# Spectral layer, expert layer and MLP on one core: the bias added after the sums, clipping and stores placed one class pair later, router logits from float32 token tiles

## The chip, the cores and the metric

The kernel runs on one core of a Trainium2 chip. The metric is the device time of one execution in microseconds (us). Three runs of the kernel before gave 3658.37, 3660.32 and 3661.04 us; the median is 3660.32 us. About 0.2% (7 us) can be told from no change in this kernel.

## The reference, cut to what matters

Three layers follow one another over eight sequences of 3072 tokens of 256 features. The first goes to the frequency domain along the sequence, multiplies by a complex 256x256 matrix, adds a complex bias, shrinks by 0.01 towards zero and goes back. The second sends each token with a positive skip score to one of eight experts. The third is a two-layer MLP with a leaky activation.

```python
X = np.fft.rfft(x, axis=1)
Yr = X.real @ w_r - X.imag @ w_i + b_r
Yi = X.real @ w_i + X.imag @ w_r + b_i
Yr = np.sign(Yr) * np.maximum(np.abs(Yr) - lam, 0.0)      # Yi likewise
x = np.fft.irfft(Yr + 1j * Yi, n=3072, axis=1)            # (8, 3072, 256)
...
xc = x[x @ w_skip > 0]
logits = xc @ w_gate                                      # 8 experts, the largest one is used
...
h = x @ w_in
return (np.maximum(h, 0.0) + alpha * np.minimum(h, 0.0)) @ w_out
```

The product with the complex matrix and the experts' products are done with float32 operands split into two float32r parts, high and low.

## The kernel before, in words

**Stages.** The transforms are factored as 3072 = 48 x 64. Stage A (`A_mm`) multiplies a 96-row input tile by a 96x96 matrix and stores the result to DRAM (`sA`). Stage B (`B_mm`) loads 128-row tiles `S` from there and multiplies by the second factor, two frequency classes at a time. `mix` multiplies by the complex weights, `shrink` adds the bias and shrinks, `C_mm` starts the way back and stores to DRAM (`sZ`), and `D_mm` finishes it into token tiles `xo`, which go to DRAM (`xb`). `T_tr` transposes each token tile, `T_mm` computes the skip score and the eight logits, `route` makes list positions of them in some ten pieces, and `scatter` writes list entries by indirect DMAs from GpSimd, 24 a batch.

**The order.** The loop runs over 97 steps; a step is one class pair of a batch (twelve pairs a batch, pair number `pp`). The schedule is written out by hand: each engine executes its instructions in the order of the program text. Step s issues the loads for s+2, then `B_mm` of pair s+1, then `T_mm` of a waiting token tile, one A, D or transposing unit as a filler, the list scatters (two a step, from step 72 four), `mix` of pair s with more fillers between its sums, `shrink` of pair s, and `C_mm` of pair s-1. A batch of inputs costs 16 A units, issued some batches ahead: two a step in pairs 11, 0, 1 and 2, one in the others, and none after step 76. A batch's 16 D units go two a step in pairs 3 to 10 of the batch after it. After the 97 steps the experts' stage begins at line 712; the last batch's D units, transposes and logits run inside it (`tail_step`).

**Three products.** For pairs other than 0, `B_three` makes three operands (`m`): real and imaginary part by one copy on ScalarE (line 213) and their sum `xs`, which is added on VectorE (line 214), rounded on ScalarE (line 215) and whose low part is taken on GpSimd (line 217). `mix_three` forms k1 from the sums and k2 and k3 from the parts. Line 232 copies k1 to `u` on ScalarE, and line 234 adds the two biases to it on GpSimd and writes `ub`. `shrink` then adds `ub` to k2 and k3 on VectorE in four 64x256 pieces (line 272), clips (274) and subtracts (275).

**Logits.** `T_tr` keeps the transposed token tile as a high part `th` (ScalarE, line 317) and a low part `tl` (VectorE, line 318). `T_mm` holds the router's weights stationary and streams 384 tokens past them four times; four tiles gather in one PSUM bank, and line 332 transposes that bank in 32x32 blocks.

**Buffers.** The pool `pa` has four PSUM banks and a step takes four (B, k1, k2 and k3 together, C), so each use gets the bank of the same use one step earlier. `pb` has three banks for A, D and transposes. `y`, `zc`, `sa` and `zin` have two buffers, `xo` and `xin` three.

Of the kernel before, what the change touches and what calls it, by code (L numbers as in the profile page):

```python
# [21 lines left out]
NQ, NP = 32, 96  # L22
# [21 lines left out]
def _constants():  # L44
# [42 lines left out]
    g, i = p // 32, p % 32  # L87
    q = 16 * (r // 12) + 4 * g + (r % 12) // 3
    tok = (X0 + SEQ * b + 32 * (32 * (r % 3) + i) + q).astype(np.float32)
# [10 lines left out]
def spectral_moe_mlp(ctx, tc, x, w_r, w_i, b_r, b_i, w_skip, w_gate, w1, w2,  # L100
# [28 lines left out]
    if True:  # L129
# [6 lines left out]
        bias = cp.tile([128, 4, D], F32, name="bias")  # L136
# [3 lines left out]
        wgw = tp.tile([128, 2, 224], F32R, name="wgw")  # L140
# [14 lines left out]
        def A_mm(b, u):  # L155
            q = bank(pb)
            nc.tensor.matmul(q[:96], agt[:, 0], xin[b, u // 2][:, 2 * (u % 2):2 * (u % 2) + 2, :], start=True, stop=True)
            if u % 2 == 0:
                sast[b] = p2.tile([96, 4, D], F32, name="sa")
            dst, src = sast[b][:, 2 * (u % 2):2 * (u % 2) + 2, :], q[:96].rearrange("p (a d) -> p a d", d=D)  # L160
            t = sast[b]
            nc.scalar.copy(dst, src)
            if u % 2 == 1:
                ch = u // 2
                for rj in range(4):
                    nc.sync.dma_start(sA[b % 3][rj, 4 * ch:4 * ch + 4].rearrange("q c d -> c q d"),
                                      t[24 * rj:24 * rj + 24])
# [34 lines left out]
        def B_three(src, m, pp):  # L202

            q = bank(pa).rearrange("p (k j i f) -> p k j i f", k=2, j=2, i=2)
            for i in range(2):
                for kt in range(2):
                    nc.tensor.matmul(q[:, kt, :, i], src[:, i, 128 * kt:128 * kt + 128], fct[:, 2 * pp + i],
                                     start=True, stop=True)
            q = q.rearrange("p k j i f -> p k j (i f)")
            xi = p2.tile([128, 2, 128], F32, name="xi", bufs=1)  # L210
            xs = p2.tile([128, 2, 128], F32, name="xs")
            nc.scalar.copy(xi, q[:, :, 1])
            nc.scalar.copy(m[:, :, 0, 0:2], q)
            nc.vector.tensor_tensor(out=xs, in0=q[:, :, 0], in1=xi, op=add)
            nc.scalar.copy(m[:, :, 0, 2], xs)  # L215
            nc.vector.tensor_tensor(out=m[:, :, 1, 0:2], in0=q, in1=m[:, :, 0, 0:2], op=sub)
            nc.gpsimd.tensor_tensor(out=m[:, :, 1, 2], in0=xs, in1=m[:, :, 0, 2], op=sub)  # L217

        def mix_three(b, pp, fill):
# [3 lines left out]
            for o, j, w in ((k1, 2, 0), (k23[:, 0], 1, 2), (k23[:, 1], 0, 1)):  # L223
# [12 lines left out]
            Y[b, pp] = (k23, ub)  # L236
# [24 lines left out]
        def shrink(b, pp):  # L261
            q = Y[b, pp]
            y = p2.tile([128, 2, D], F32, name="y")
            if pp == 0:
                for i in range(2):
                    nc.vector.tensor_tensor(out=y[:, i], in0=q[:, i], in1=bias[:, 3 - i], op=add)
            else:
                q, ub = q
                for i in range(2):
                    for j in range(2):  # L270
                        r = slice(64 * i, 64 * i + 64)
                        nc.vector.tensor_tensor(out=y[64 * j:64 * j + 64, i], in0=q[r, j], in1=ub[r, j], op=add)  # L272
# [3 lines left out]
            Y[b, pp] = y  # L276

        def C_mm(b, pp):
# [5 lines left out]
            nc.scalar.copy(z, q)  # L284
            for rj in range(4):
# [8 lines left out]
        def D_mm(b, u):  # L294
# [7 lines left out]
            if u % 2 == 1:  # L302
                nc.sync.dma_start(
                    xb[X0 + SEQ * b:X0 + SEQ * b + SEQ].rearrange("(p q) d -> p q d", q=NQ)[:, 4 * ch:4 * ch + 4, :], t)
# [3 lines left out]
        def T_tr(b, ch, kt):  # L308
            src = xo[b, ch]
            if kt == 0:  # L310
                xt[b, ch] = (t2.tile([128, 2, 384], F32R, name="th", bufs=1),
                             t2.tile([128, 2, 384], F32R, name="tl", bufs=1))
            h, l = xt[b, ch]
# [3 lines left out]
            nc.scalar.copy(h[:, kt], q[:, :384])  # L317
            nc.vector.tensor_tensor(out=l[:, kt], in0=q[:, :384], in1=h[:, kt], op=sub)

        def T_mm(b, ch):  # L320
            h, l = xt.pop((b, ch))
            g = ch % 4
            if g == 0:
                lgt[b] = bank(pc)
            q = lgt[b][:, :384]
            for kt in range(2):
                wv = wgw[:, kt, 96 - 32 * g:224 - 32 * g]
                nc.tensor.matmul(q, wv, h[:, kt], start=(g == 0 and kt == 0), stop=False)
                nc.tensor.matmul(q, wv, l[:, kt], start=False, stop=(g == 3 and kt == 1))
            if g == 3:  # L330
                lt = t2.tile([128, 12, 32], F32, name="lt")
                nc.vector.transpose(out=lt.rearrange("p a c -> p (a c)"), in_=q)
                if ch == 3:
                    sal[b] = t2.tile([128, 24, 9], F32, name="sal")
                nc.vector.tensor_tensor(out=sal[b][:, 3 * ch - 9:3 * ch + 3], in0=lt[:, :, 0:9], in1=lt[:, :, 9:18], op=add)
# [247 lines left out]
        def setup0():  # L583
# [7 lines left out]
            nc.sync.dma_start(bias[:, 0], bcast(b_r, 128))  # L591
            nc.sync.dma_start(bias[:, 1], bcast(b_i, 128))
            nc.sync.dma_start(bias[0:64, 2], bcast(b_r, 64))
            nc.sync.dma_start(bias[64:128, 2], bcast(b_i, 64))
            nc.sync.dma_start(bias[0:65, 3], bcast(b_r, 65))
            nc.sync.dma_start(bias[65:128, 3], bcast(b_i, 63))
# [7 lines left out]
        def setup2():  # L604
            V = nc.vector
            for kt in range(2):
                V.tensor_copy(wgw[:, kt], zero[:, 0:224])
            V.tensor_copy(wgw[:, :, 96:105], gst)
            V.tensor_tensor(out=wgw[:, :, 105:114], in0=gst, in1=wgw[:, :, 96:105], op=sub)
# [8 lines left out]
            pad = padt[0] = t2.tile([128, LS // 256, 3], I32, name="pad", tag="th", bufs=1)  # L618
# [23 lines left out]
        for i in range(16):  # L642
# [4 lines left out]
            A_mm(0, i)  # L647
        S_load(0, 0)
# [6 lines left out]
        for s in range(NS + 1):  # L655
# [6 lines left out]
            if s % 3 == 0:  # L662
                const_load(2)
            for k in a_at.get(s + 2, []):
# [7 lines left out]
            if s + 1 < NS:  # L672
                B_mm(*bp(s + 1))
            trail_mm()
# [22 lines left out]
            trail_route(1)  # L697
            if routed[0] == BR and not ev:
# [12 lines left out]
    if True:  # L711
# [418 lines left out]
        def tail_step():  # L1130

            trail_mm()
# [202 lines left out]
```

## Time and profile before

| | before |
|---|---|
| median of three runs | 3660.32 us |
| the profiled execution, its own time | 3661.88 us |
| span of its profile | 3660.2 us |
| TensorE busy in the span | 3427.4 us (94%) |
| VectorE, ScalarE, GpSimd busy | 2550.1, 2054.0, 1892.8 us |
| first stage (the 97 steps), from the span's start | about 62 to 872 us |
| experts' stage, MLP | about 872 to 1575 us, 1575 to 3660 us |

The profiled execution is 1.6 us (0.04%) above the median. A busy TensorE counts modelled ends of pipelined matmuls, so it says where the engine is idle rather than how near its peak it is; its own pace is read from the starts of the same matmul in successive steps. The granted clock of TensorE stands as a share of 2.4 GHz.

### The profile page before, as it was taken

The page shows a single profiled execution, that of the slowest core. Times are in us where ns is not written, and L with a number is a line of the kernel's source. Part 1 is how long each engine was busy: PE and PEld are TensorE (multiplying, and loading weights), DVE is VectorE, ACT ScalarE, POOL GpSimd, SP SyncE. Part 2 cuts the span into 40 slices and gives each one's busy share as a digit, 9 for nine tenths or more (in the row PEclk, how much of TensorE's full clock was granted, in tenths as well). Part 3 has the DMA queues.
Part 4 walks back from the last instruction along what each step waited for, and adds up shares of the span by engine and source line. Part 5 has one row for each costly group of instructions (what it writes and reads, how often), then busy time and mean ns, then how long its engine had stood idle before and what let it go on. Part 6 is the DMA issues. An engine that isn't in the chain of part 4 may idle for free.

```text
span 3660.2 us, 48950 instructions
## 1 busy us (share of the span) xinstructions
PE 3427.4 (94%) x16110; PEld 2733.6 (75%) x16110; DVE 2550.1 (70%) x4206; ACT 2054.0 (56%) x3995; POOL 1892.8 (52%) x1602
## 2 busy tenths in 40 slices
PE   6999889777889999989999999999999999999998
PEld 4777667566668888867777777777777777777776
DVE  2666666465437878877777777777777777777775
ACT  2454444333324333346676766767676766666765
POOL 1223444534556656635555555555555555555554
PEclk8999999888989999999999999999999999999999
DMA  7876666444322232221111111111111111111101
GB/s 203 242 213 183 185 193 171 127 114 124 87 62 90 86 96 86 81 43 24 24 24 24 24 24 24 33 32 24 29 24 24 24 24 24 24 24 24 24 12 25
DMA packets 354703, 267.32 MB, mean 73 GB/s; under 512 B 245597, under 2 KB 322750, under 8 KB 354438
## 3 DMA queue, kind: packets, MB, share of 16 engines
q1 hardware_dynamic: 337766, 234.74, 25.1%
q0 software_dynamic: 16672, 29.35, 2.8%
q8 instruction: 129, 2.11, 0.3%
q14 instruction: 136, 1.11, 0.1%
HBM read 148.09 MB, written 117.00 MB: 72 GB/s over the span
## 4 chain that ended last, share of the span: by engine, by line
PE 54%; DVE 15%; POOL 10%; issue 10%; ACT 5%; DMA 3%; another core or an unknown queue 1%; SPq 1%; POOLq 0%; DVEq 0%; ACTq 0%
PE bank L1002 19%; PE bank L950 17%; PE bank L825 5%; PE bank L844 4%; DVE xf L889 3%; POOL lst L451 3%; DVE y L272 2%; POOL wex L885 2%; POOL gl L991 2%; PE bank L227 2%; PE bank L845 2%; PE bank L296 2%; DVE wex L885 2%; POOL ub L234 2%; DMA xin<-in_x 1%
## 5 line engine op out<-in xcount | busy, mean ns | idle before, releaser
L991 POOL TENSOR_TENSOR gl<-P,gh 128x512 fp32r<-128x512 f32 x768 | 1041.7, 1371 | 920.1 <-ACT gh L990 776.0
L950 PE MATMUL bank<-wex,wi 128*128 128x512 f32 x4032 | 1023.7, 398 | 25.9 <-DVE C L963 13.4
L1002 PE MATMUL bank<-gh,wo 128*128 128x512 f32 x3072 | 965.9, 395 | 0.0
L950 PEld LDWEIGHTS bank<-wex,wi 128*128 128x128 f32 x4032 | 747.9, 188 | 241.0 <-DVE C L963 23.8
L1002 PEld LDWEIGHTS bank<-gh,wo 128*128 128x128 f32 x3072 | 575.9, 188 | 142.3 <-issue 0.8
L983 DVE SCALAR_TENSOR_TENSOR P<-R,al,P 128x512 f32<-128x512 f32 x768 | 582.9, 774 | 105.5 <-ACT R L982 102.9
L1002 PE MATMUL bank<-gl,wo 128*128 128x512 f32 x1536 | 607.0, 395 | 0.0
L990 ACT CAST gh<-P 128x512 fp32r<-128x512 f32 x768 | 449.5, 616 | 169.6 <-PE bank L1002 169.6
L981 ACT ACTIVATE P<-C 128x512 f32<-128x512 f32 x576 | 358.4, 622 | 170.8 <-DVE C L973 155.2
L973 DVE TENSOR_TENSOR C<-bank,u 128x512 f32<-128x512 f32 x384 | 255.1, 683 | 170.7 <-PE bank L950 169.0
L982 ACT ACTIVATE R<-C 128x512 f32<-128x512 f32 x576 | 355.4, 617 | 0.0
L227 PE MATMUL bank<-wri,m 128*128 128x256 f32 x1584 | 310.2, 337 | 43.9 <-DVE y L272 43.0
L1002 PEld LDWEIGHTS bank<-gl,wo 128*128 128x128 f32 x1536 | 288.0, 188 | 70.7 <-POOL gl L991 0.2
L227 PEld LDWEIGHTS bank<-wri,m 128*128 128x128 f32 x1584 | 225.9, 198 | 145.3 <-issue 125.9
L844 PE MATMUL bank<-wex,gh 128*128 128x512 f32 x824 | 306.0, 402 | 26.1 <-DVE os L862 23.9
L828 ACT ACTIVATE gh<-bank 128x512 fp32r<-128x512 f32 (+1 forms) x232 | 128.0, 552 | 332.1 <-PE bank L825 256.0
L217 POOL TENSOR_TENSOR m<-xs,m 128x256 fp32r<-128x256 f32 x88 | 64.5, 732 | 450.5 <-ACT m L215 449.8
L825 PE MATMUL bank<-xTh,wex 128*128 128x512 f32 (+1 forms) x928 | 279.1, 382 | 6.7 <-issue 3.0
L272 DVE TENSOR_TENSOR y<-bank,ub 64x256 f32<-64x256 f32 x352 | 148.5, 422 | 194.4 <-POOL ub L234 188.4
L981 ACT ACTIVATE P<-bank 128x512 f32<-128x512 f32 x192 | 115.0, 599 | 260.6 <-PE bank L950 257.6
L829 DVE SCALAR_TENSOR_TENSOR gl<-bank,gh 128x512 fp32r<-128x512 f32 (+1 forms) x232 | 145.2, 626 | 156.8 <-ACT gh L828 123.6
L962 DVE TENSOR_TENSOR u<-bank,u 128x512 f32<-128x512 f32 x192 | 132.9, 692 | 161.9 <-ACT u L961 155.7
(185 smaller groups left out, 5178.2 us busy)
## 6 DMA issues: line engine op xcount, KB each, us to landing
xin<-in_x SPq DMA_DIRECT2D x64, 384.0 KB
sA<-sa SPq DMA_DIRECT2D x256, 96.0 KB
sZ<-zc SPq DMA_DIRECT2D x384, 64.0 KB
zin<-sZ SPq DMA_DIRECT2D x64, 384.0 KB
xb<-xo SPq DMA_DIRECT2D x64, 384.0 KB
xr<-xb SPq DMA_DIRECT2D x192, 128.0 KB
out<-os SPq DMA_DIRECT2D x192, 128.0 KB
S<-sA SPq DMA_DIRECT2D x31, 768.0 KB
```

The lines of the kernel that those rows point to most:

```text
L227: nc.tensor.matmul(o, m[:, kt, xa, j], wri[:, wa, w, kt], start=(n == 0), stop=(n == 5))
L272: nc.vector.tensor_tensor(out=y[64 * j:64 * j + 64, i], in0=q[r, j], in1=ub[r, j], op=add)
L825: nc.tensor.matmul(q, a, b[:, kt, :N], start=(i == 0), stop=(i == 5))
L844: nc.tensor.matmul(o, gh[:, 128 * a:128 * a + 128], w, start=(f == 0), stop=False)
L950: nc.tensor.matmul(o[:, :n], w[:, k, m], b, start=(first and i == 0), stop=(i == 2), skip_group_check=True)
L973: V.tensor_tensor(out=C[:, i], in0=q[2 + i][:, :n], in1=u, op=add)
L981: nc.scalar.activation(g, src, AF.Relu)
L982: nc.scalar.activation(R, src, AF.Relu, scale=-1.0)
L983: V.scalar_tensor_tensor(out=g, in0=R, scalar=mlp['al'][:, 2 * c + f:2 * c + f + 1], in1=g, op0=mult, op1=add)
L990: nc.scalar.copy(gh[:, :n], P[f][:, t, :n])
L991: nc.gpsimd.tensor_tensor(out=gl[:, :n], in0=P[f][:, t, :n], in1=gh[:, :n], op=sub)
L1002: nc.tensor.matmul(oacc[j][t][h], w[:, k, 128 * h:128 * h + 128], b, start=(f + i == 0), stop=(f == NF - 1 and i == 2))
```

## The change

- `mix_three` no longer makes `ub`. A new `gather`, at the end of `mix`, adds `u` to k2 and k3 on VectorE (line 284 of the changed kernel) and then adds the bias in place on GpSimd (line 285). For pair 0 it adds the bias on VectorE as before.
- `shrink` keeps only the clip and the subtraction and is called one step later, behind `B_mm` of the next step.
- The rounding of `xs` and its low part move to `B_sum`, behind the step's first filler.
- The stores of A, C and D results are put on lists and issued at the head of the next step (`store`), C's ahead of the others.
- `T_tr` keeps one float32 tile `xt` with two buffers; the low part's subtraction goes. `T_mm` holds 128 tokens stationary and streams nine columns of router weights: six float32 matmuls a tile, into one bank a batch. At a batch's last tile one copy takes the bank to `sal`; the 32x32 transposes and the sum behind them go. The table of token numbers follows the new layout.

```diff
+        def A_store(b, ch, t):
+            for rj in range(4):
+                nc.sync.dma_start(sA[b % 3][rj, 4 * ch:4 * ch + 4].rearrange("q c d -> c q d"), t[24 * rj:24 * rj + 24])
...
+        def store():
+            while stores:
+                stores.pop(0)()
...
-            nc.scalar.copy(m[:, :, 0, 2], xs)
             nc.vector.tensor_tensor(out=m[:, :, 1, 0:2], in0=q, in1=m[:, :, 0, 0:2], op=sub)
-            nc.gpsimd.tensor_tensor(out=m[:, :, 1, 2], in0=xs, in1=m[:, :, 0, 2], op=sub)
+            sums.append((xs, m))
+        def B_sum():
+            while sums:
+                xs, m = sums.pop()
+                nc.scalar.copy(m[:, :, 0, 2], xs)
+                nc.gpsimd.tensor_tensor(out=m[:, :, 1, 2], in0=xs, in1=m[:, :, 0, 2], op=sub)
...
-                    ub = p2.tile([128, 2, D], F32, name="ub")
-                    nc.gpsimd.tensor_tensor(out=ub, in0=u.rearrange("p (o d) -> p o d", o=1).to_broadcast([128, 2, D]),
-                                            in1=bias[:, 0:2], op=add)
...
+        def gather(b, pp):
+            q = Y[b, pp]
+            y = Y[b, pp] = p2.tile([128, 2, D], F32, name="y")
...
+            for i in range(2):
+                for j in range(2):
+                    r = slice(64 * i, 64 * i + 64)
+                    nc.vector.tensor_tensor(out=y[64 * j:64 * j + 64, i], in0=q[r, j], in1=u[r], op=add)
+            nc.gpsimd.tensor_tensor(out=y, in0=y, in1=bias[:, 1:2].to_broadcast([128, 2, D]), op=add)
...
+            stores.insert(0, lambda: C_store(b, pp, z))
...
-            nc.scalar.copy(h[:, kt], q[:, :384])
-            nc.vector.tensor_tensor(out=l[:, kt], in0=q[:, :384], in1=h[:, kt], op=sub)
+            nc.scalar.copy(xt[b, ch][:, kt], q[:, :384])
...
-                nc.tensor.matmul(q, wv, h[:, kt], start=(g == 0 and kt == 0), stop=False)
-                nc.tensor.matmul(q, wv, l[:, kt], start=False, stop=(g == 3 and kt == 1))
+            for i in range(3):
+                for kt in range(2):
+                    nc.tensor.matmul(lgt[b][:, 3 * ch + i], t[:, kt, 128 * i:128 * i + 128], gst[:, kt],
+                                     start=(kt == 0), stop=(kt == 1))
...
+            store()
             for k in a_at.get(s + 2, []):
                 a_need(*k)
...
             if s + 1 < NS:
                 B_mm(*bp(s + 1))
+            if s:
+                shrink(*bp(s - 1))
             trail_mm()
...
             fill()
+            B_sum()
             trail_scatter(2 if s < 72 else 4)
...
                 mix(b, pp, fill)
-                shrink(b, pp)
+                gather(b, pp)
```

VectorE, a step in the middle of a batch, from `xs` to the next step's `xs`. Before:

```order
L214 TENSOR_TENSOR xs<-bank,xi 128x256
L216 TENSOR_TENSOR m<-bank,m 128x2x256
L318 TENSOR_TENSOR tl<-bank,th 128x384 x2
L272 TENSOR_TENSOR y<-bank,ub 64x256 x4
L274 TENSOR_SCALAR cl<-y 128x512
L275 TENSOR_TENSOR y<-y,cl 128x512
L214 TENSOR_TENSOR xs<-bank,xi 128x256
```

The same place in the change:

```order
L220 TENSOR_TENSOR xs<-bank,xi 128x256
L221 TENSOR_TENSOR m<-bank,m 128x2x256
L290 TENSOR_SCALAR cl<-y 128x512
L291 TENSOR_TENSOR y<-y,cl 128x512
L284 TENSOR_TENSOR y<-bank,u 64x256 x4
L220 TENSOR_TENSOR xs<-bank,xi 128x256
```

The clip and the subtraction now belong to the pair before and stand ahead of the four sums; the two subtractions of `tl` are gone.

TensorE, the head of a step with logits, from B's matmuls to the transposes. Before:

```order
L207 MATMUL bank<-fct,S 128x2x64 x4
L328 MATMUL bank<-th,wgw 128x384
L329 MATMUL bank<-tl,wgw 128x384
L328 MATMUL bank<-th,wgw 128x384
L329 MATMUL bank<-tl,wgw 128x384
L157 MATMUL bank<-xin,agt 96x512
L227 MATMUL bank<-wri,m 128x256 x6
L316 MATMUL bank<-ident,xo 128x96 x4
```

The same place in the change:

```order
L213 MATMUL bank<-fct,S 128x2x64 x4
L341 MATMUL bank<-gst,xt 128x9 x6
L155 MATMUL bank<-xin,agt 96x512
L241 MATMUL bank<-wri,m 128x256 x6
L332 MATMUL bank<-ident,xo 128x96 x4
```

Four matmuls of 384 columns became six of nine columns; nothing else moved on TensorE.

SyncE's queue in the second batch, two steps with D units (`zin` and `xin` are loads, the others stores). Before:

```order
L292 DMA zin<-sZ_62 96x1024
L303 DMA xb<-xo 96x1024
L286 DMA sZ_63<-zc 32x2x256 x4
L292 DMA zin<-sZ_62 96x1024
L166 DMA sA_61<-sa 24x4x256 x4
L286 DMA sZ_63<-zc 32x2x256 x4
L303 DMA xb<-xo 96x1024
L153 DMA xin<-in_x 96x1024
```

The same place in the change:

```order
L310 DMA zin<-sZ_62 96x1024
L304 DMA sZ_63<-zc 32x2x256 x4
L321 DMA xb<-xo 96x1024
L310 DMA zin<-sZ_62 96x1024
L304 DMA sZ_63<-zc 32x2x256 x4
L166 DMA sA_61<-sa 24x4x256 x4
L321 DMA xb<-xo 96x1024
L151 DMA xin<-in_x 96x1024
```

Between the same loads stand the same stores; within a step C's four stores (`sZ`) moved ahead of A's (`sA`) and D's (`xb`).

## Rows read from the trace of the kernel before

**Rows 1.** Stretches: span, busy time by engine, granted TensorE clock, DMA share, GB/s.

```profile
62.00:220.00 158.00, 151.49 (x903) 117.26 (x903) 97.77 (x211) 81.01 (x182) 45.20 (x47) 1.00 0.80 233
220.00:627.00 407.00, 366.04 (x2108) 282.09 (x2108) 249.93 (x571) 191.97 (x427) 162.88 (x164) 0.97 0.67 187
627.00:872.00 245.00, 186.13 (x1009) 151.21 (x1009) 137.12 (x320) 82.64 (x191) 115.05 (x115) 0.87 0.43 113
872.00:1100.00 228.00, 185.78 (x906) 153.00 (x906) 99.20 (x224) 76.01 (x154) 115.33 (x119) 0.89 0.36 94
```

**Rows 2.** Who waited for whom, 220 to 872 us: total, times, longest.

```profile
POOL m L217 <- ACT m L215: 309.7, 65, 9.3
...
DVE y L272 <- POOL ub L234: 155.4, 50, 6.9
```

**Rows 3.** Timeline of GpSimd, a step with four scatters: start, duration, idle before.

```profile
813.10 0.72 POOL L217 TENSOR_TENSOR m<-xs,m 128x256 fp32r<-128x256 f32 x1 [3.99 <-ACT m L215]
813.98 1.00 POOL L451 DMA_INDIRECT lst<-pay,di  x1 [0.15 <-issue]
...
818.85 1.31 POOL L234 TENSOR_TENSOR ub<-u,bias 128x512 f32<-128x512 f32 x1
824.15 0.73 POOL L217 TENSOR_TENSOR m<-xs,m 128x256 fp32r<-128x256 f32 x1 [3.99 <-ACT m L215]
```

**Rows 4.** Timeline of VectorE in the same step.

```profile
820.19 1.73 DVE L272 TENSOR_TENSOR y<-bank,ub 64x256 f32<-64x256 f32 x4 [4.65 <-POOL ub L234]
...
823.14 0.42 DVE L214 TENSOR_TENSOR xs<-bank,xi 128x256 f32<-128x256 f32 x1
```

**Rows 5.** Timeline of ScalarE in the same step.

```profile
823.60 0.41 ACT L215 CAST m<-xs 128x256 fp32r<-128x256 f32 x1 [5.16 <-DVE xs L214]
```

**Rows 6.** Timeline of TensorE: starts of B's matmuls in some steps, and what follows.

```profile
112.91 1.05 PE L207 MATMUL bank<-fct,S 128*128 128x128 f32 x8
...
119.36 1.05 PE L207 MATMUL bank<-fct,S 128*128 128x128 f32 x8
...
188.85 1.05 PE L207 MATMUL bank<-fct,S 128*128 128x128 f32 x8
189.66 0.42 PE L328 MATMUL bank<-th,wgw 128*128 128x384 f32 x1
...
190.44 0.59 PE L157 MATMUL bank<-xin,agt 96*96 96x512 f32 x1
...
196.75 1.05 PE L207 MATMUL bank<-fct,S 128*128 128x128 f32 x8
...
219.60 1.05 PE L207 MATMUL bank<-fct,S 128*128 128x128 f32 x8
...
226.63 1.05 PE L207 MATMUL bank<-fct,S 128*128 128x128 f32 x8
...
318.74 1.05 PE L207 MATMUL bank<-fct,S 128*128 128x128 f32 x8
...
324.35 1.05 PE L207 MATMUL bank<-fct,S 128*128 128x128 f32 x8
...
871.15 0.80 PE L282 MATMUL bank<-y,cct 128*128 128x256 f32 x1 [1.39 <-DVE y L275]
```

**Rows 7.** Timeline of TensorE's weight loads, B's and the transposes'.

```profile
196.87 0.75 PEld L207 LDWEIGHTS bank<-fct,S 128*128 128x128 f32 x6
197.53 0.19 PEld L328 LDWEIGHTS bank<-th,wgw 128*128 128x128 f32 x1
...
199.82 0.41 PEld L316 LDWEIGHTS bank<-ident,xo 96*128 96x128 f32 x4
200.17 0.30 PEld L227 LDWEIGHTS bank<-wri,m 128*128 128x128 f32 x2
```

**Rows 8.** Groups of ScalarE's instructions, 220 to 872 us: busy, mean ns, idle before.

```profile
L162 ACT COPY sa<-bank 96x512 f32<-96x512 f32 x72 | 40.2, 577 | 0.0
```

**Rows 9.** Timeline of SyncE's queue: one step's stores of C.

```profile
816.66 1.74 SPq L286 DMA_DIRECT2D sZ<-zc  x4
```

More of the change, by code (lines that the diff above doesn't have):

```diff
@@ L135, in spectral_moe_mlp @@
         wri = cp.tile([128, 2, 4, 2, D], F32R, name="wri")
-        bias = cp.tile([128, 4, D], F32, name="bias")
+        bias = cp.tile([128, 2, D], F32, name="bias")
         zero = cp.tile([128, 256], F32, name="zero")
@@ L163, in A_mm @@
             if u % 2 == 1:
[L164 to L167, printed above, removed]
+                stores.append(lambda: A_store(b, u // 2, t))
+        def A_store(b, ch, t):
+            for rj in range(4):
+                nc.sync.dma_start(sA[b % 3][rj, 4 * ch:4 * ch + 4].rearrange("q c d -> c q d"), t[24 * rj:24 * rj + 24])
+        stores = []
+        def store():
+            while stores:
+                stores.pop(0)()
         S, M, Y, zc = {}, {}, {}, {}
@@ L259, in mix, with shrink @@
             Y[b, pp] = q
-        def shrink(b, pp):
+        def gather(b, pp):
             q = Y[b, pp]
-            y = p2.tile([128, 2, D], F32, name="y")
+            y = Y[b, pp] = p2.tile([128, 2, D], F32, name="y")
             if pp == 0:
                 for i in range(2):
[L266 to L272, printed above, removed]
+                    nc.vector.tensor_tensor(out=y[:, i], in0=q[:, i], in1=bias[:, i], op=add)
+                return
+            q, u = q
+            for i in range(2):
[3 more added lines that the diff above has]
+            nc.gpsimd.tensor_tensor(out=y, in0=y, in1=bias[:, 1:2].to_broadcast([128, 2, D]), op=add)
+        def shrink(b, pp):
+            y = Y[b, pp]
             cl = p2.tile([128, 2, D], F32, name="cl", bufs=1)
@@ L316, in T_tr @@
                 nc.tensor.transpose(q[:, 96 * i:96 * i + 96], src[:, i, 128 * kt:128 * kt + 128], ident[:96, :96])
-            nc.scalar.copy(h[:, kt], q[:, :384])
-            nc.vector.tensor_tensor(out=l[:, kt], in0=q[:, :384], in1=h[:, kt], op=sub)
+            nc.scalar.copy(xt[b, ch][:, kt], q[:, :384])
         def T_mm(b, ch):
[L321 to L327, printed above, removed]
-                nc.tensor.matmul(q, wv, h[:, kt], start=(g == 0 and kt == 0), stop=False)
-                nc.tensor.matmul(q, wv, l[:, kt], start=False, stop=(g == 3 and kt == 1))
[L330 to L335, printed above, removed]
+            t = xt.pop((b, ch))
+            if ch == 0:
+                lgt[b] = bank(pc)[:, 0:216].rearrange("p (a e) -> p a e", e=9)
+            for i in range(3):
+                for kt in range(2):
+                    nc.tensor.matmul(lgt[b][:, 3 * ch + i], t[:, kt, 128 * i:128 * i + 128], gst[:, kt],
+                                     start=(kt == 0), stop=(kt == 1))
+            if ch == 7:
+                sal[b] = t2.tile([128, 24, 9], F32, name="sal")
+                nc.vector.tensor_copy(sal[b], lgt.pop(b))
         def route(b):
@@ L590, in setup0 @@
             V.tensor_tensor(out=wri[:, 1], in0=wst, in1=wri[:, 0], op=sub)
[L591 to L596, printed above, removed]
+            nc.sync.dma_start(bias[0:65, 0], bcast(b_r, 65))
+            nc.sync.dma_start(bias[65:128, 0], bcast(b_i, 63))
+            nc.sync.dma_start(bias[0:64, 1], bcast(b_r, 64))
+            nc.sync.dma_start(bias[64:128, 1], bcast(b_i, 64))
         def setup1():
@@ L605, in setup2 @@
             V = nc.vector
[L606 to L609, printed above, removed]
             V.memset(scan[0], 0.0)
```

25 lines of the change are left out of this document (13 added, 12 removed).

## Prediction

> **What bounds the kernel now.** I read the stretches first. TensorE is busy for 151 of 158 us up to 220 us, at the full clock; then for 366 of 407 and 186 of 245 us, at a granted clock of 0.97 and 0.87 [rows 1]. So the first stage loses its time after 220 us, and the clock (full is 2.4 GHz, the other level 1.2 GHz) falls where TensorE idles. The change touches nothing behind that stage but the last batch's logits.
>
> Second, the waits of 220 to 872 us. The reader should see a ring: GpSimd waits 309.7 us for ScalarE's rounding, VectorE 155.4 us for GpSimd's `ub` [rows 2]. The timeline of one step closes it. From 813.10 us GpSimd takes the low part of the sums, four list scatters and `ub`, and is done at 820.16 [rows 3]; VectorE then adds `ub`, clips and subtracts before it comes to the next `xs` at 823.14 [rows 4]; ScalarE rounds that at 823.60 [rows 5]; and GpSimd starts again at 824.15 [rows 3]. One turn is 11.05 us, and nothing in it is TensorE's. A scatter with its gap is (818.85 - 813.98) / 4 = 1.22 us, so the turn is 8.6 us with two scatters and 6.2 us with none. That is why the step is clean before the first scatters and long behind them.
>
> Third, TensorE's own pace. From B's start to B's start a step with D units and one A is 196.75 - 188.85 = 7.90 us, one with two A and logits 226.63 - 219.60 = 7.03 us, one with two A alone 324.35 - 318.74 = 5.61 us [rows 6]. All three have TensorE's matmuls back to back.
>
> **What the ring costs.** A batch has seven steps of the first kind, three near the second (pairs 11, 0 and 3) and two of the third: 7 x 7.90 + 3 x 7.03 + 2 x 5.61 = 87.6 us. From 219.60 us six batches remain: 526 us. Of their A units 24 are missing at the end; at B's pace of 0.11 us for 128 columns [rows 7] an A (two passes of 512 columns) is 0.88 us, so 21 us go off: 505 us. Measured are 871.15 - 219.60 = 651.5 us [rows 6], of which 1.5 us are the closing step. So 145 us are waits and slow clock.
>
> **The change, part by part.**
>
> *Bias behind the sums, shrink a step later.* VectorE's sums need only `u`, which ScalarE copies in mid-step, so they no longer wait for the scatters. GpSimd adds the bias behind them, as long as `ub` took (1.31 us, same width [rows 3]), and what waits for that is the clip of the next step, queued behind `xs` there. Who is queued behind it? The same step's four sums, which wait for `mix` anyway, and C, at the step's end. GpSimd's own load with four scatters stays at 7.06 us; TensorE's step then, without A, is 7.90 - 0.88 + 0.54 (below) = 7.56 us. So TensorE becomes the bound. Steps 5 to 11 have no scatters, but two A: one is 119.36 - 112.91 = 6.45 us [rows 6], where 5.61 is TensorE's; some six of them give 5 us.
>
> Not all of the 145 us go. Steps 84 to 86 have neither A nor (two of them) logits, some 5 us of matmuls, less than GpSimd's 7.06 us; and the routing's pieces on VectorE still come between. Unknown: nothing may stay, or half (73 us). I take 20 us, nearer to nothing, because the clean steps of 7.90 us carry the same work of VectorE and ScalarE without a wait.
>
> *The sums' rounding behind the first filler.* ScalarE no longer stands before `xs` with fillers queued behind it; TensorE needs the operand a step later. Counted above.
>
> *Logits.* Four matmuls of 384 columns took 190.44 - 189.66 = 0.78 us [rows 6]. Now each tile has six float32 matmuls of nine columns; a float32 matmul runs as two passes with a weight load each (B's four make eight records [rows 6]), so twelve loads of 128 columns with almost nothing to stream. The trace shows no such matmul. Below: the transposes' loads, spaced (200.17 - 199.82) / 4 = 0.088 us: 1.06 us. Above: a load's full 0.19 us, nothing overlapped: 2.28 us. Nearest is B, float32 128x128 loads like these, (197.53 - 196.87) / 6 = 0.11 us apart [rows 7]: 1.32 us, 0.54 us more than now. There are 64 tiles: 48 in the six batches (+26 us), 8 before 220 us and 8 in the experts' stage (+4 us each). Ends: +18 and +96 us for all.
>
> The Trainium skill's page "TensorE: Matmul & The Clock Gate" has two rules that part here. Its section "Back-to-back issue gap" gives about 60 cycles to any matmul of up to 64 columns; by that alone, an estimate, twelve take 0.3 us and the sum would come out near 3498 us. Its section "LDWEIGHTS" charges a load by its columns, 128 / 1.2 = 107 ns, which gives 1.28 us and leaves the sum within 3 us of mine. B's spacing cannot part load from stream, since both are 128 columns; no run here shows nine columns yet.
>
> *The low part and the 32x32 transposes go.* 1.1 us a tile leave VectorE. It is not the bound in a clean step: nothing.
>
> *Stores a step later.* In SyncE's queue they are not later. The queue holds only its own instructions, and between the same loads stand the same stores; C's just went ahead of A's. C's result comes last in a step, so A's stores go out later by up to C's four, 1.74 us [rows 9], and ScalarE needs A's buffer again two tiles on. Its copies of `sa` had no idle time before them [rows 8]. Nothing, at most 1 us in each of some 38 steps with two A.
>
> **The sum.** -145 + 20 (waits that stay) + 26 + 4 + 4 (logits) - 5 (early steps) = -96 us. The profiled execution took 3661.9 us, 1.6 above the median of 3660.3; against the median that is 3564 us.
>
> **Rivals.**
>
> *A. GpSimd keeps the ring, shifted.* The clip waits for the bias add, which stands behind the scatters; the four sums stand behind the clip. For: GpSimd's 7.06 us against 7.56 leave little room. Against: from the bias add to the next rounding VectorE and ScalarE need only clip, sums and `xs`, under 4 us [rows 4, 5], beside the scatters and not after them. If half of the waits stay: 3564 + 53 = 3617 us.
>
> *B. The clock falls.* Nine-column matmuls leave TensorE all but idle in each step. For: 0.87 where it idled 59 of 245 us. Against: 1.00 where it idled 7 of 158 [rows 1], and a logits block is 1.3 us in 8.4. At 0.87 over the new 530 us: +79 us, 3643 us. The Trainium skill's page "TensorE: Matmul & The Clock Gate", section "Loop structure matters more than you think", says likewise that gaps between matmul bursts bring the clock back to the lower level. By that rule the freed waits should raise it: the rows agree as far as they go.
>
> *C. A's stores hold ScalarE* by 1 us in the 38 steps: 3602 us.
>
> *D. Slower.* Each nine-column matmul must end before the next weight load begins. Place: the logits block at a step's head, in front of the fillers. Price: 0.19 us of load and 0.28 us of matmul (eight in 1.05 us at 0.11 [rows 6]) make 0.47 us a pair, 5.6 us a block, 4.9 us more than now on 64 tiles: +312 us in place of +34, so 3842 us. It turns slower from 0.24 us a pair on. Against: B's loads start while the matmul ahead of them runs [rows 7].
>
> *E. No change:* the ring isn't what holds TensorE, only what the others wait on. Against it: 7.90 us in clean steps and 11.05 in that one.
>
> **Chances.** Forecast 0.70, A 0.11, B 0.06, C 0.06, D 0.04, E 0.03. The range reaches down to all waits gone and the cheap loads (3564 - 20 - 16 = 3528) and up to A, and the dear loads (3564 + 62 = 3626): 3527 to 3630 us. Within 0.2% (7 us, about what the measurement can tell) lies E, 0.03; slower is D and a part of the unforeseen, 0.05; faster 0.92.
>
> **What would show it.** Right: no wait of VectorE's sums for GpSimd; B's starts 8.4 us apart in steps with D, A and logits, 7.6 without A; granted clock near 1.00 to the stage's end, which comes at about 775 us; the rest as long as before. Wrong in its size: blocks of other than 1.3 us; VectorE's clip waiting for GpSimd with C behind it (A); clock under 0.95 in clean steps (B); ScalarE's `sa` waiting for a DMA (C).

## The result and the profile after

The changed kernel takes 3574.93 us (median of four runs, 3573.73 to 3579.98) where the kernel before, on the same chip, takes 3660.68 us. The ratio is 0.9767 with an interval of 0.9751 to 0.9784: 85.7 us faster. Forecast were 3564 us in a range of 3527 to 3630.

| | before | after | difference |
|---|---|---|---|
| span of the profile | 3660.2 us | 3573.9 us | -86.3 |
| start of step 1 | 62.2 | 59.3 | -2.9 |
| steps 1 to 11 | 70.0 | 75.1 | +5.1 |
| steps 12 to 23 | 87.4 | 90.1 | +2.7 |
| steps 24 to 71 | 407.9 | 371.3 | -36.6 |
| steps 72 to the last C | 245.1 | 187.3 | -57.8 |
| behind the last C | 2787.6 | 2790.8 | +3.2 |

The steps are cut at B's first matmul, as in [rows 6], and at the start of C's last one; step s is the loop's step s, in which B of pair s+1 is issued. The row for the start of step 1 is no effect of the change that can be told: in the control below, the same program, step 1 starts at 59.9 us, in the other variants of it between 57.0 and 63.8. The first rows to compare are the stretches of the changed kernel, cut at the same steps as [rows 1] (span, busy time of TensorE, weight loads, VectorE, ScalarE, GpSimd, granted clock, DMA share, GB/s):

```profile
62.00:224.00 162.00, 152.74 (x934) 120.92 (x933) 88.29 (x187) 81.39 (x178) 45.78 (x46) 0.98 0.77 221
224.00:596.00 372.00, 368.35 (x2374) 295.88 (x2374) 239.49 (x498) 202.82 (x430) 171.35 (x164) 1.00 0.74 205
596.00:783.00 187.00, 168.92 (x1143) 142.60 (x1142) 121.95 (x280) 85.93 (x190) 120.47 (x115) 0.99 0.57 151
783.00:1011.00 228.00, 192.09 (x944) 158.14 (x944) 85.94 (x194) 74.61 (x152) 114.96 (x119) 0.87 0.35 93
```

The second stretch is now TensorE's: 368.35 busy of 372, at the full clock where 0.97 was granted before. The third went from 0.87 to 0.99. The first got worse: 0.98 for 1.00, and four microseconds longer. The last is as it was.

Who waited for whom, 224 to 783 us (in total, times, longest), against [rows 2]:

```profile
POOL m L231 <- ACT m L230: 136.8, 60, 5.6
POOL y L285 <- DVE y L284: 90.6, 42, 7.2
...
DVE cl L290 <- POOL y L285: 27.0, 15, 3.7
...
PE bank L297 <- DVE y L291: 14.3, 11, 2.9
```

No wait of VectorE's four sums for GpSimd is left. In its place stands the clip's, 27.0 us in 15 steps where `ub` cost 155.4 in 50. TensorE's C waits 14.3 us for the subtraction behind the clip; how much of that comes from the clip's wait and how much from the routing's pieces on VectorE was not parted. GpSimd still waits for the rounding, but now because it is done early.

A four-scatter step on GpSimd, against [rows 3] (start, duration, what, idle time before):

```profile
623.96 0.93 POOL L231 TENSOR_TENSOR m<-xs,m 128x256 fp32r<-128x256 f32 x1 [2.76 <-ACT m L230]
625.04 1.26 POOL L461 DMA_INDIRECT lst<-pay,di  x1 [0.16 <-issue]
...
630.17 1.30 POOL L285 TENSOR_TENSOR y<-y,bias 128x512 f32<-128x512 f32 x1
631.40 0.74 POOL L231 TENSOR_TENSOR m<-xs,m 128x256 fp32r<-128x256 f32 x1
```

and VectorE and ScalarE in it, against [rows 4, 5]:

```profile
623.89 0.42 DVE L290 TENSOR_SCALAR cl<-y 128x512 f32<-128x512 f32 x1
...
626.56 1.66 DVE L284 TENSOR_TENSOR y<-bank,u 64x256 f32<-64x256 f32 x4
628.50 0.42 DVE L220 TENSOR_TENSOR xs<-bank,xi 128x256 f32<-128x256 f32 x1 [0.27 <-issue]
...
631.50 0.94 DVE L290 TENSOR_SCALAR cl<-y 128x512 f32<-128x512 f32 x1 [1.98 <-POOL y L285]
```

```profile
628.95 0.41 ACT L230 CAST m<-xs 128x256 fp32r<-128x256 f32 x1
```

The next `xs` is added at 628.50 and rounded at 628.95, while GpSimd still scatters: its next low part starts at 631.40, straight behind the bias. The ring is open. VectorE's clip waits 1.98 us, with only the step's own sums and C behind it.

The logits block, TensorE's matmuls and then its weight loads in the same step (start, duration):

```profile
191.30 1.05 PE L213 MATMUL bank<-fct,S 128*128 128x128 f32 x8
192.19 1.41 PE L341 MATMUL bank<-gst,xt 128*128 128x9 f32 x12
193.45 1.08 PE L155 MATMUL bank<-xin,agt 96*96 96x512 f32 x2
...
199.81 0.39 PE L213 MATMUL bank<-fct,S 128*128 128x128 f32 x2
```

```profile
192.08 1.42 PEld L341 LDWEIGHTS bank<-gst,xt 128*128 128x128 f32 x12
193.42 0.25 PEld L155 LDWEIGHTS bank<-xin,agt 96*96 96x96 f32 x2
```

Six matmuls make twelve records. Their loads follow one another by (193.42 - 192.08) / 12 = 0.112 us, 1.34 us a block. From B to B the step is 199.81 - 191.30 = 8.51 us where it was 7.90.

One place is worse, step 11, from B at 119.87 us on. TensorE, ScalarE's copies of `sa` (no idle time before them in [rows 8], and up to 220 us of the kernel before 1.2 us of waits for a store of `sa`; 28.8 us in 12 waits in the change) and SyncE's queue:

```profile
119.87 1.05 PE L193 MATMUL bank<-fct,S 128*128 128x128 f32 x8
127.04 2.02 PE L155 MATMUL bank<-xin,agt 96*96 96x512 f32 x2 [6.12 <-DMA xin<-in_x]
...
134.35 1.05 PE L213 MATMUL bank<-fct,S 128*128 128x128 f32 x8
```

```profile
124.02 0.58 ACT L160 COPY sa<-bank 96x512 f32<-96x512 f32 x1 [8.37 <-DMA sA<-sa]
```

```profile
113.15 1.93 SPq L629 DMA_DIRECT2D lst<-pad  x4
115.12 4.66 SPq L304 DMA_DIRECT2D sZ<-zc  x4
120.59 1.57 SPq L166 DMA_DIRECT2D sA<-sa  x4
122.26 0.33 SPq L151 DMA_DIRECT2D xin<-in_x  x1
```

The step takes 14.48 us where some 6.4 were usual. ScalarE waits 8.37 us for the store of `sa`; that store was issued from 120.59 on, behind four list fills (`lst`) and C's four stores (`sZ`, which took 4.66 us for 1.74 in [rows 9]). TensorE then waits 6.12 us for `xin`, which stands behind A's stores, and comes back at the lower clock level (granted 0.5 from 125.5 to 132.3 us): its two passes of 512 columns take 2.02 us for 1.08.

### The profile page after: what moved, and what is told of

Its sections match the earlier page's. It is cut to its first block, busy times and chain, and to the rows that moved or that the text cites. A ratio compares the mean times of both kernels' runs of the same rounds, so it can differ in the third digit from the quotient of the medians.

```text
span 3573.9 us, 49794 instructions
## 1 busy us (share of the span) xinstructions
PE 3429.1 (96%) x16622; PEld 2755.3 (77%) x16622; DVE 2506.3 (70%) x4050; ACT 2069.3 (58%) x3995; POOL 1903.9 (53%) x1602
## 4 chain that ended last, share of the span: by engine, by line
PE 64%; DVE 12%; issue 8%; POOL 7%; ACT 4%; DMA 2%; another core or an unknown queue 1%; SPq 1%; POOLq 0%; DVEq 0%; ACTq 0%
PE bank L1013 19%; PE bank L961 17%; PE bank L836 5%; PE bank L241 4%; PE bank L855 4%; DVE xf L900 3%; PE bank L314 3%; PE bank L155 3%; POOL wex L896 2%; POOL gl L1002 2%; PE bank L297 2%; PE bank L341 2%; PE bank L213 2%; PE bank L856 2%; DVE wex L896 2%
## 5 line engine op out<-in xcount | busy, mean ns | idle before, releaser
L241 PEld LDWEIGHTS bank<-wri,m 128*128 128x128 f32 x1584 | 218.1, 191 | 90.1 <-issue 87.1
L856 PE MATMUL bank<-wex,gl 128*128 128x256 f32 x824 | 235.1, 285 | 7.5 <-DVE gl L840 7.3
L284 DVE TENSOR_TENSOR y<-bank,u 64x256 f32<-64x256 f32 x352 | 148.4, 422 | 128.7 <-PE bank L241 83.8
```

The costliest lines, as they stand in the source:

```text
L241: nc.tensor.matmul(o, m[:, kt, xa, j], wri[:, wa, w, kt], start=(n == 0), stop=(n == 5))
L856: nc.tensor.matmul(o[:, 0:256], gl[:, 128 * a:128 * a + 128], w[:, 0:256], start=False, stop=(f == NFE - 1))
```

## The experiments

The theory after these readings: the whole gain is the opened ring; the float32 logits cost more than they give; and a queue of SyncE in which fills overtake stores spoils steps 9 to 11. Each kernel was measured beside the kernel before on its own chip. Where that one takes 3625 to 3627 us, the difference given is from the changed kernel there (the control, 3537.76 us); where it takes 3660.7 us, from 3574.93 us. With ratio intervals of about 0.0013 either way, a difference of two such ratios shows from some 7 us on.

| kernel | time, us | ratio to before (95%) | from the changed kernel |
|---|---|---|---|
| control: the change again | 3537.76 | 0.9756 [0.9743, 0.9770] | |
| old logits | 3514.42 | 0.9692 [0.9678, 0.9707] | -23 |
| before, new logits only | 3636.10 | 1.0027 [1.0017, 1.0038] | |
| shrink in its own step | 3574.25 | 0.9856 [0.9841, 0.9871] | +36 |
| bias first | 3645.18 | 0.9964 [0.9952, 0.9976] | +70 |
| sums rounded inline | 3570.45 | 0.9755 [0.9743, 0.9768] | -4 |
| bias and shrink alone | 3539.48 | 0.9670 [0.9658, 0.9683] | -35 |
| A's stores first | 3536.52 | 0.9753 [0.9739, 0.9766] | -1 |
| fills later | 3525.36 | 0.9728 [0.9715, 0.9741] | -12 |
| fills behind the stores | 3532.61 | 0.9750 [0.9737, 0.9764] | -5 |
| logits of 64 columns | 3537.08 | 0.9760 [0.9747, 0.9774] | -1 |
| old logits, A first, fills later | 3499.63 | 0.9658 [0.9644, 0.9671] | -38 |

**The control.**

> The changed kernel itself, beside the next three on the same chip. Every theory: 0.977 of the kernel before, as in the first measurement (-85.7 us); step 11 near 14.5 us, clean steps with D, A and logits at 8.51 us.

As expected: step 11 took 14.28 us, clean steps 8.51. The last matmul of C starts at 783.3 us, in the first profile at 783.1; the 37 us between the two chips lie behind it (last section).

**Old logits in the changed kernel.** `T_tr`, `T_mm`, `wgw` and the table of token numbers as before the change.

```diff
-    nc.tensor.matmul(lgt[b][:, 3 * ch + i], t[:, kt, 128 * i:128 * i + 128], gst[:, kt], ...)
+    nc.tensor.matmul(q, wv, h[:, kt], start=(g == 0 and kt == 0), stop=False)
+    nc.tensor.matmul(q, wv, l[:, kt], start=False, stop=(g == 3 and kt == 1))
```

> The changed kernel with the logits of before: split token tiles, four matmuls of 384 columns, 32x32 transposes. Theory (TensorE is now the bound, and a block of nine-column matmuls costs it about 0.6 us more): steps with D units, one A and logits at 7.9 us instead of 8.51, steps without A at 7.0 instead of 7.65; 64 blocks x 0.6 = 38 us off, 3537 us. Rival (the low-part subtractions on VectorE, 1.1 us a step, come back into the path now that VectorE's sums follow TensorE closely): steps stay near 8.5 us and the time within 7 us of 3575.

23 us faster than the change. The clean steps return to 7.90 and 7.04 us and step 11 stays at 14.03, so the logits' price is on TensorE and has nothing to do with the early steps. But 64 blocks at 0.61 us are 39 us: some 15 didn't come. Steps in which VectorE also works on the routing stayed longer than the clean ones: steps 31 and 32 took 8.46 and 8.29 us (8.51 both in the change), and 85 and 86 took 7.01 and 6.46 where the control has 5.88 and 5.57. In step 31 TensorE's transposes wait for the low part's subtraction:

```profile
275.46 0.55 PE L336 MATMUL bank<-ident,xo 96*128 96x96 f32 x4 [0.33 <-DVE tl L338]
```

By the steps of the two traces, 4 us of the missing ones are lost in steps 24 to 71, 7 from step 72 on and 3 behind the last C. That the subtractions cause all of it is not shown: with the old logits the 32x32 transposes on VectorE and single buffers for `th` and `tl` came back too.

**New logits in the kernel before.** The same edit the other way round.

> The kernel before with the new logits alone. Theory (the ring through GpSimd sets the steps with scatters and has no TensorE in it): the 0.6 us a block hides in steps with scatters and shows only in the clean ones, some 20 of 56, and in the experts' stage: 3670 us, 3660 to 3680. Rival 1 (TensorE paces all steps): +38 us, 3698 us. Rival 2 (VectorE's two subtractions were part of the ring): 1.1 us off each of the some 40 steps with scatters and logits, 3625 us.

9.5 us slower than before (interval 6 to 14), within what the theory gave; both rivals are out. Where the ring sets the step, most of the 0.6 us more of TensorE's time is hidden: the same edit costs 10 us in front of a waiting TensorE and 23 in front of a full one. That is why parts can't simply be added.

**Shrink in its own step.** Bias behind the sums as changed, but clip and subtraction called directly behind it.

```diff
-            if s:
-                shrink(*bp(s - 1))
...
                 gather(b, pp)
+                shrink(b, pp)
```

> The changed kernel with the clip and subtraction called right behind the bias add, in the same step. Theory (what broke the ring is that nothing on VectorE ahead of the next sums waits for GpSimd): the clip again waits for the add behind the scatters, and the next xs stands behind the clip: one turn is 7.06 us of GpSimd plus clip, subtraction, xs and rounding, about 2.2 us, so 9.3 us with four scatters (7.56 to 7.65 now) and 6.9 with two (8.5 now, TensorE's): only the 18 steps with four scatters grow, by 1.7 us, 3605 us. Rival (putting the sums ahead of the bias add was enough, since C needs the result a step later): 3575 us, within 7.

36 us slower, where 30 were expected. Steps 78, 79 and 81 to 83 take 9.22 to 9.27 us. GpSimd's timeline has the turn (start, duration, idle before), and VectorE's what closes it:

```profile
687.95 0.73 POOL L231 TENSOR_TENSOR m<-xs,m 128x256 fp32r<-128x256 f32 x1 [2.22 <-ACT m L230]
...
693.67 1.31 POOL L285 TENSOR_TENSOR y<-y,bias 128x512 f32<-128x512 f32 x1
697.22 0.72 POOL L231 TENSOR_TENSOR m<-xs,m 128x256 fp32r<-128x256 f32 x1 [2.23 <-ACT m L230]
```

```profile
695.02 0.43 DVE L290 TENSOR_SCALAR cl<-y 128x512 f32<-128x512 f32 x1 [4.80 <-POOL y L285]
695.49 0.69 DVE L291 TENSOR_TENSOR y<-y,cl 128x512 f32<-128x512 f32 x1
696.21 0.42 DVE L220 TENSOR_TENSOR xs<-bank,xi 128x256 f32<-128x256 f32 x1
```

697.22 - 687.95 = 9.27 us: the ring of before [rows 3 to 5] without its four sums (1.73 us). With two scatters, 2.4 us less, such a turn is below TensorE's 8.51, and the steps with D, A and logits kept that time. Step 72 starts when it does in the control (597.5 and 597.6 us).

**Bias first.** The other half undone: `ub` made behind the scatters, the sums wait for it, the shrink stays a step later.

```diff
+                    nc.gpsimd.tensor_tensor(out=ub, in0=u.rearrange(...).to_broadcast([128, 2, D]), in1=bias[:, 2:4], op=add)
...
-                    nc.vector.tensor_tensor(out=y[64 * j:64 * j + 64, i], in0=q[r, j], in1=u[r], op=add)
-            nc.gpsimd.tensor_tensor(out=y, in0=y, in1=bias[:, 1:2].to_broadcast([128, 2, D]), op=add)
+                    nc.vector.tensor_tensor(out=y[64 * j:64 * j + 64, i], in0=q[r, j], in1=ub[r, j], op=add)
```

> The bias goes back to its old place (GpSimd makes ub from u behind the scatters, VectorE's sums wait for it); the shrink stays one step later. Theory (each of the two edits cuts only a part of the ring): the turn is the old 11.05 us less clip and subtraction (1.5 us), 9.5 us; steps from 78 with four scatters at 9.5 to 10.1 us where the changed kernel has 7.65, steps with two scatters (7.1 us) unchanged at 8.51; 30 to 40 us above the changed kernel, 0.985 of before. Rival (the later shrink alone opens the ring, the order of bias and sums is nothing): within 5 us of the changed kernel.

70 us slower, twice what was expected; of the change's gain some 15 us are left. The direction holds and the rival is out, the size is not right. The turn on GpSimd:

```profile
687.68 0.93 POOL L231 TENSOR_TENSOR m<-xs,m 128x256 fp32r<-128x256 f32 x1 [2.80 <-ACT m L230]
688.77 1.26 POOL L463 DMA_INDIRECT lst<-pay,di  x1 [0.16 <-issue]
...
693.90 1.30 POOL L248 TENSOR_TENSOR ub<-u,bias 128x512 f32<-128x512 f32 x1
698.00 0.93 POOL L231 TENSOR_TENSOR m<-xs,m 128x256 fp32r<-128x256 f32 x1 [2.80 <-ACT m L230]
...
701.87 0.99 POOL L463 DMA_INDIRECT lst<-pay,di  x1 [1.52 <-issue]
...
709.54 0.93 POOL L231 TENSOR_TENSOR m<-xs,m 128x256 fp32r<-128x256 f32 x1 [2.80 <-ACT m L230]
```

It is 10.32 us, not 9.5. Clip and subtraction took 1.19 us out of it, not 1.5 (GpSimd idles 2.80 us for 3.99 [rows 3]), and the low part takes 0.93 us for 0.72 and the first scatter 1.26 for 1.00, while clip and subtraction run on VectorE. The next turn is 11.54 us, from 698.00, and the difference of 1.22 us is one scatter, at 701.87, which GpSimd starts 1.52 us behind the one ahead of it instead of 0.30; the profile shows nothing that it waits for, and why stays open. Beside the ring, C now waits for a late shrink, and the clock falls: 38 us at the lower level between 627 us and the last C, 5 in the control. Also outside it, step 1 starts 4.5 us later than in the change. Steps with scatters and routing in the middle batches rose too (steps 38 and 39 took 9.73 and 7.91 us, 6.81 and 6.69 in the change). Undone singly the two edits cost 36 and 70 us. The order of bias and sums is the larger part, the late shrink the smaller, and each alone leaves a ring that is shorter (9.3 and 10.3 us for 11.05) but still longer than TensorE's 7.65.

**Sums rounded inline.** `B_sum()` called at the end of B instead of behind the first filler.

> The rounding of xs and its low part go back into B, ahead of the first filler; all else as changed. Theory (ScalarE has slack, this part is no carrier of the gain): clean steps stay at 8.51 us and the time within 7 us of the changed kernel, 0.976 of the kernel before. Rival (ScalarE then stands before xs while the filler's copy is queued behind it, and the filler's bank comes free late): half a us or more in some 80 steps, 40 us and more above the changed kernel, 0.987.

Within 5 us of the change, clean steps 8.51 us. This part carries nothing that can be told.

**Bias and shrink alone.** The change without its logits, its late rounding and its late stores.

> Only the new bias add behind the sums and the shrink one step later; logits, rounding of the sums and places of the stores as before the change. Theory (these two edits cut the ring and carry the whole gain, the stores' move made the long step 11): no waits of VectorE's sums for GpSimd, clean steps 7.90 us, steps 6 to 11 near 6.4 us each as in the kernel before, sum 38 to 42 us instead of 47; 3508 us on this chip where before takes 3625, 0.967. Rival (the later stores or the later rounding are needed too): steps with scatters over 9 us again and a ratio above 0.975.

0.967, as expected: two of the change's five edits carry more than its whole gain, 121 us of which the others give 35 back. Steps 6 to 11 take 38.4 us together (46.7 in the change, 40.7 before), although the sixteen fills stand in the same four steps. So the fills alone are not the cause.

**A's stores first.** On the list of stores, C's go behind A's.

```diff
-            stores.insert(0, lambda: C_store(b, pp, z))
+            stores.append(lambda: C_store(b, pp, z))
```

> The changed kernel with C's stores behind A's and D's in each step's list instead of ahead of them. Theory (in steps 6 to 12, with two A a step and the list fills on the same queue, A's stores wait behind C's and ScalarE waits for their landing, up to 8.4 us): these waits of ScalarE for the stores of sa, 28.8 us in all, go, step 11 falls from 14.5 to about 6 us, and the time is 8 to 12 us shorter, 3565 us. Rival (the queue is late by its own length, fills included, whatever the order): nothing changes, 3575 us.

A miss: step 11 takes 12.21 us for 14.28, but the time is the control's within the interval. The prediction's rival C, in the form in which it stood there (C's four stores ahead of A's), does not make the stall. It may carry a small part of it: steps 6 to 11 take 43.6 us for the control's 47.8, and the last C comes 4.5 us earlier, less than the times can tell.

**Fills later.** One fill a step in steps 12 to 27.

```diff
-            for i in range(4 * (s - 7), 4 * (s - 6)):
-                if 0 <= i < 16:
-                    fill_list(i)
+            if 12 <= s < 28:
+                fill_list(s - 12)
```

> The sixteen stores that pre-fill the lists go one a step in steps 12 to 27 instead of four a step in steps 7 to 10. Theory (SyncE's queue holds thirteen DMAs and more in a step of 5.6 us, about 0.45 us each, so A's stores and xin loads behind them run late and the steps pay it back in 9 to 11): no step of 6 to 11 over 7 us; these six, 46.7 us in the changed kernel, come to 34 to 36 us, so 11 to 13 us less than the changed kernel (ratio to before 0.9735). Rival (the order alone makes the stall, C's four stores ahead of A's): step 11 stays above 12 us and the time within 4 us of the changed kernel.

As expected: 12 us, and steps 6 to 11 at 35.5 us in sum, 6.75 the longest. The waits of ScalarE's `sa` copies for a store between 90 and 140 us fall from 20.7 to 3.0 us.

**Fills behind the stores.** The same fills in the same steps, but the `store()` call ahead of them.

> Only the list fills of steps 7 to 10 change place in SyncE's queue: behind the stores of the step before, as the kernel before has them, instead of ahead of them. Theory (the change let four fills overtake the stores of A, and that made the long step 11): no step of 7 to 11 over 8 us, six steps 6 to 11 at 38 to 40 us instead of 47, 0.973 to 0.974 of the kernel before. Rival (not the overtaking, but that the stores stand ahead of the next loads of xin): step 11 again over 12 us, 0.976.

Steps 6 to 11 take 39.4 us and the longest 8.03, much as the theory says, and the last C ends 7.8 us earlier than in the control. The time fell by only 5 us, less than can be told; steps 12 and 14 take back 2 us. So the overtaking made the long step. It is not the whole: TensorE still waits 4.8 us for `xin` in steps 10 to 12, and ScalarE 17.6 us for stores of `sa` between 90 and 140 us. In the kernel with bias and shrink alone, which has the same fills but issues each store in its own step, these waits are 1.1 and 1.8 us. So the later stores cost something themselves as long as the fills are in the queue.

**Logits of 64 columns.** The router's weights padded with 55 columns of zeros.

```diff
-                    nc.tensor.matmul(lgt[b][:, 3 * ch + i], ...
+                    nc.tensor.matmul(lgt[b][:, 27 * ch + 9 * i:27 * ch + 9 * i + 64], ...
```

> The router's weights padded from nine to 64 columns, the 55 new ones zero, each overwritten by the next block's matmul, so only the streamed width changes. Theory (the block's 1.34 us are its twelve weight loads, and nine columns stream underneath them): the block stays at 1.34 us, the time within 5 us of the changed kernel. Rival (load and stream follow one another): 55 columns more, at most 0.11 us for 128, are up to 0.047 us on each of twelve, 0.57 us a block and 36 us on 64 tiles: ratio to before 0.987, clean steps 9.1 us.

TensorE's matmuls and loads in this kernel:

```profile
192.60 1.45 PE L341 MATMUL bank<-gst,xt 128*128 128x64 f32 x12
193.89 1.05 PE L155 MATMUL bank<-xin,agt 96*96 96x512 f32 x2
```

```profile
192.49 1.42 PEld L341 LDWEIGHTS bank<-gst,xt 128*128 128x128 f32 x12
193.83 0.25 PEld L155 LDWEIGHTS bank<-xin,agt 96*96 96x96 f32 x2
```

Again 193.83 - 192.49 = 1.34 us; the steps are 8.53 us for 8.51. Seven times the columns cost next to nothing: the block goes at the pace of its twelve loads.

**Old logits, A first, fills later.** The three together.

> Three edits of the changed kernel together: logits as before the change, C's stores behind A's, the list fills one a step in steps 12 to 27. If the parts add up: -28 us for the logits and -12 us for the early steps, so 40 us less than the changed kernel, 0.966 of the kernel before, the fastest so far. If the early steps were no cost of their own (time saved there returns as a later wait): 0.969, as with the old logits alone.

3499.63 us, 38 less than the change and 125 less than the kernel before on that chip: the fastest of all. The parts (23, 1 and 12 us) added up.

## Why the prediction was right, point by point

**The ring: right, by its place and its size.** The prediction took 145 us of waits out and 20 back. From step 24 to the last C the time fell by 653.0 - 558.6 = 94.4 us. With 48 logits blocks at 0.61 us (29 us) put aside, 123.7 us of waits went, where 125 were forecast. Of the steps the prediction's own floor (87.6 us a batch, plus 8 blocks) gives 92.5 us; steps 36 to 47 take 92.9. Nearly all the waits that stay, some 22 us by that floor, lie behind step 72. TensorE idles 18 us there: 5.5 in steps 74 to 76, 1.0 in step 80, 1.3 in step 83, 5.9 in steps 85 to 87 and 3.8 in the last ones. The prediction had named steps 84 to 86, but with a bound that isn't theirs: they take 5.97, 5.91 and 5.58 us, less than GpSimd's 7.06, since no scatter is left in them (GpSimd's timeline has none from 686 to 713 us). TensorE waits there for the shrink, which on VectorE stands behind the routing's pieces, the prediction's other reason. The 20 us themselves were picked between 0 and 73, and that 22 came is luck in the size. The two experiments that undo one edit each, and the one that has these two edits alone, show that this is the cause.

**Logits: the row chosen was the right one, the price 0.07 us a step low.** B's 0.11 us a load was nearest; 0.112 was measured, 1.34 us a block where 1.32 was forecast. The step grew by 0.61 us instead of 0.54: 0.56 between B's start and the first A (193.45 - 191.30 = 2.15 for 190.44 - 188.85 = 1.59 [rows 6]) and the rest in that A itself, which takes 0.52 us to the next matmul where 0.46 were usual (190.90 - 190.44 in the kernel before). That is some 4.5 us on 64 tiles. Rival D is out with 0.112 us a pair against its 0.47. Of the two rules that the prediction weighed, these blocks bear out the one of the section "LDWEIGHTS" in the Trainium skill's page "TensorE: Matmul & The Clock Gate" (an estimate of 107 ns for 128 columns; 112 measured), though the transposes' loads, at 0.088 us [rows 7], are quicker than it. The figure in the section "Back-to-back issue gap" of the same page of the Trainium skill (about 60 cycles up to 64 columns) would have given an estimated 0.3 us a block where 9 and 64 columns both take 1.34. That section of the Trainium skill says itself that the figure leaves the weight loads out, so the two were no rivals for a stream in which each matmul has its own load.

**The work that leaves VectorE: a term set to nothing that was worth up to 15 us.** "It is not the bound in a clean step: nothing" is true of clean steps. In steps where the routing's pieces run on VectorE it is false, as the kernel with old logits shows: a block saves 0.61 us in clean steps, but all 64 save 23 us rather than 39. The size is that difference, rests on two medians, and is shared by the subtractions, the 32x32 transposes and the single buffers in a way that was not parted.

**The early steps: wrong, and the step that failed was a sentence.** Forecast were -5 us for steps 5 to 11; steps 1 to 11 took 5.1 us more, so this term is some 10 us off. "Between the same loads stand the same stores" compared loads and stores alone, and [rows 8], which were to bear it out, begin at 220 us, behind the steps in question. The list fills of steps 7 to 10 are issued at a step's head too, and the change put the stores behind them: in the kernel before A's stores were ahead of the next fills, in the change behind them. Chance C (0.06) had the right symptom, ScalarE waiting for the store of `sa`, in 12 steps rather than 38, with a wrong cause. Three kernels part them: order of A and C, no effect on the time that can be told; fills behind the stores, step 11 at 8.03 us; fills elsewhere, no long step at all.

**The other steps.** The late rounding was counted at nothing and is nothing. The clip's wait for GpSimd (rival A) exists, 27.0 us in 15 steps, and didn't close a ring again, for the reason that the prediction gave: what stands behind it before the next rounding runs beside GpSimd's next scatters (from the clip at 631.50 us the subtraction and the sums are done by 634.8, while GpSimd scatters from 632.31 on). Rival B fell: the nine-column blocks came with a granted clock of 1.00 and 0.99 for 0.97 and 0.87. Up to the last C the clock fell where TensorE had waited, in the long step 11 and once in step 88, and nowhere in steps 24 to 71. The section "Loop structure matters more than you think" of the Trainium skill's page "TensorE: Matmul & The Clock Gate" points the same way as these rows. The last C came at 783 us instead of about 775, mainly by the early steps and the dearer logits; what followed took as long as before, within 3.2 us where 4 were forecast.

## What to carry to other kernels

Where an engine works 7 us of an 11 us step and is still on the path, follow its waits from engine to engine until they close, and take the work of one of them out of that loop; here two edits did it, and the other three together cost 35 us more than they gave. A matmul of few columns cost its weight load here (0.112 us for 9 as for 64 columns), and four matmuls of 384 columns with the weights stationary were cheaper than six of nine (0.78 us for 1.34): where TensorE is the bound, count loads before columns. When an issue moves within an in-order queue, list everything in that queue at that place, the one-off transfers of the start-up too.

## What had not been expected of the hardware

- VectorE's clip and subtraction and GpSimd's work slow each other when they run at once, and the one that starts second pays. In the change the clip at 623.89 us took 0.42 us, GpSimd's low part that began 0.07 us behind it 0.93 for 0.72, and the first scatter, beside the subtraction, 1.26 for 1.00. At 631.40 us the low part came first and took 0.74 us, and the clip 0.10 us behind it 0.94; at 695.02 us of the kernel with the shrink in its own step, where GpSimd was idle, it took 0.43. Not every pair does this: in the kernel before, low parts that ran wholly beside VectorE's 32x32 transposes or the routing's pieces took 0.73 to 0.75 us. A step that overlaps the former kind pays some tenths of a microsecond.
- Two chips differed by one per cent in one stage alone. The changed kernel took 3574.93 us on the first chip and 3537.76 on another, with the last C at 783.1 and 783.3 us; all of the 36 us between the two profiles lie behind it, in the experts' stage: the MLP's first matmul starts at 1493.9 and at 1457.7 us. On the first, ScalarE's waits between 783 and 1000 us include these (in total, times, longest), on the other none with that releaser:

```profile
ACT gh L839 <- remote: 30.8, 5, 10.8
...
ACT xt L333 <- remote: 6.5, 1, 6.5
...
ACT xo L319 <- remote: 4.6, 1, 4.6
```

The kernel before, some 35 us slower on the first chip too, shows 36.6 us of such waits in its own experts' stage. All five kernels profiled where the kernel before takes 3660.7 us have them (25 to 42 us), and none of the nine profiled elsewhere has any. What holds ScalarE there was not tried, and whether it is the whole difference stays open. Two kernels should be timed on the same chip.
